# Attention block with a gated MLP on one core: VectorE's 32x32 turns for q's last 64 columns, and mean and scale of tiles 6 to 8 through DRAM

## The chip, the cores and the metric

The kernel runs on one core of one Trainium2 chip. A core has five engines that each work through a queue of their own in order: PE (TensorE, matrix products), DVE (VectorE), ACT (ScalarE), POOL (GpSimd) and SP (SyncE, which here issues nearly all DMAs). An instruction that waits for a semaphore holds up everything behind it on its engine. The metric is the time of one execution in microseconds (us); lower is better.

## The reference

The input x has 2048 rows of 576 numbers. Each row is normalized (mean and variance), then goes through two branches: a linear attention with 32 heads of 18 columns, and a gated MLP of width 4608. The output is x + s * silu(B).

```python
xn = (x - mean) / sqrt(var + 1e-5)
q, k, v = heads(xn @ wqkv)                        # 32 heads of 18
phi = lambda t: where(t > 0, t + 1, exp(t)) + 1e-6
kv  = einsum("hsd,hse->hde", phi(k), v);  z = sum over s of phi(k)
o   = (phi(q) @ kv) / (phi(q) . z + 1e-6)
s   = o @ wo
B   = (gelu(xn @ w_gate) * (xn @ w_up)) @ w_down
out = x + s * silu(B)
```

All of it is float32.

## The kernel before

The 2048 rows are cut into 16 tiles of 128 (n or t in the code) and into 4 blocks of 512 rows (tb, 4 tiles each, TT = 4). Matrix products of float32 are made as sums of products of two shorter words, "hi" (a rounded copy, made by ACT) and "lo" (the rest, made by DVE as source minus hi), so that each operand is cut once and PE runs 7 passes for one product.

The attention branch comes first and takes some 275 us; the MLP follows with a long run of matrix products. In the attention branch:

- `kv_tile(t)` makes tile t's 1152 columns of k and v (and, in the third of its three products, 64 columns of q) by three groups of 14 matmuls into banks `kv_0`, `kv_1`, `kv_2`. Between them it prepares tile t + 1: `turn` and `place`. Every second tile, `kv_pair` adds the last two tiles to the sum kv.
- For tiles 4 and up x is loaded already turned (columns on partitions). `spread` and `scales` work out mean and scale of a pair of tiles per row, with rows on partitions (tiles `bn`, `mv`, `st`). `normalize` (called by `place`) needs them with rows along the free dimension, the same on all partitions. Up to tile 8 `turn` gives this: two PE transposes of a broadcast column, into a bank `ms`. For tiles 9 and up `scales` writes four numbers per row to DRAM (`md`), a second DMA reads them back to all partitions (`mx`), and `sort_rows` has ACT copy them into order (`mr`).
- `normalize` is then a subtraction and two multiplications on DVE (tiles `x`, `xf_B`), two ACT copies (hi) and four DVE subtractions (lo) into `xo_B`, which the next tile's matmuls read.
- phi of q is needed with columns on partitions, in 5 groups of 128 rows (gi) for each block. Groups 0 to 3 come from 14 matmuls of 512 columns each (`q_mm`, bank `q_0` to `q_3`). Group 4 holds q's last 64 columns, which `v_post` has copied from `kv_2` into `qt`, twice side by side; four PE transposes turn them into bank `q_4`. Then `phi`: ACT makes relu(-q) (`e_q`), DVE makes max(q, 0) + eps (`ph`), ACT makes the exponential of `e_q`, POOL adds. In every `phi` DVE's step waits for ACT's first one, which reads the same bank.
- Blocks 0 and 1 store phi(q) to DRAM (`q_store`), blocks 2 and 3 keep it (`q_hold`). `den` sums the denominators of a block (PE), takes the reciprocal and spreads it into `aux` (DVE and ACT), and `scale` multiplies it in by a matmul (bank `b`).

What stands between the matmuls of q is set by the tables `behind` and `ahead`, keyed by (block, group): an entry runs after the matmuls and the phi of that group are issued. All compute instructions keep the order in which the code issues them; the pools hand out buffers in that order (`gl` has 6, `tmp` has 4, and `bank` has 6 PSUM banks).

Of the kernel before, what the change touches and what calls it, by code (L numbers as in the profile page):

```python
# [8 lines left out]
F32 = mybir.dt.float32  # L9
# [3 lines left out]
ALU = mybir.AluOpType  # L13
# [78 lines left out]
def block_kernel(ctx, tc, x, xe, xt, wq_d, wkv_d, wo, wgu_d, wd_d, out):  # L92
# [21 lines left out]
    def gl_tile(shape, name, dt=F32):  # L114
        return sb.tile(shape, dt, tag="gl", bufs=6, name=name)
# [6 lines left out]
    def act(*args, **kw):  # L122
        pin(nc.scalar.activation(*args, **kw))  # L123
# [61 lines left out]
    def scales(n0):  # L185

        n, mv, st = mom.pop(n0)
        v, r, c = (st[:, i, 0:n] for i in range(1, 4))
        if n == 1:
            vec("tensor_scalar", c, r, r, -0.5, op0=ALU.mult, op1=ALU.mult)  # L190
            vec("tensor_scalar", c, c, v, 1.5, op0=ALU.mult, op1=ALU.add)
            vec("tensor_scalar", c, c, r, None, op0=ALU.mult)
        else:
            vec("scalar_tensor_tensor", c, r, -0.5, r, op0=ALU.mult, op1=ALU.mult)
            vec("tensor_mul", c, c, v)
            vec("scalar_tensor_tensor", c, c, 1.5, r, op0=ALU.add, op1=ALU.mult)
        for t in range(n):
            scale_of[n0 + t] = mv[:, t, 0:1], c[:, t : t + 1]
        if n0 >= 2 * TT:
            vec("tensor_copy", st[:, 3, 2:4], mv[:, 0:2, 0])  # L200
            d = dr.tile([P, 4], F32, name=f"md_{n0}")
            mixed[n0] = g = gl_tile([P, P, 4], f"mx_{n0}")
            dma(out=d, in_=st[:, 3, :])
            dma(
                out=g.rearrange("p t c -> p (t c)"),
                in_=d.rearrange("t c -> (t c)")[None, :].to_broadcast([P, 4 * P]),
            )

    def sort_rows(n0):

        g = gl_tile([P, 4, P], f"mr_{n0}")
        act(g, mixed.pop(n0).rearrange("p t c -> p c t"), AF.Copy)
        for t in range(2):
            if n0 + t > 2 * TT:
                rows_of[n0 + t] = [g[:, None, i + t] for i in (2, 0)]

    def center(n):

# [267 lines left out]
    def v_post(t, c):  # L486

        if c == 1:
            vas[t] = slot([P, 2 * NHG, P // 2], F32, f"va_{t}")
            pool("memset", vas[t][:, :, 0:1], 1.0)  # L490
        va, src = vas[t], pkv[t, c]
        n = D - TW[0] if c == 1 else 0
        g = 4 * c - 4
        act(
            va[:, g : g + 4, 1 : GW // 2 + 1],
            src[:, n : n + 2 * GW].rearrange("p (g j) -> p g j", g=4), AF.Copy,
        )
        if c == 2:
            act(
                va[:, 8:10, 1 : W4 // 2 + 1],  # L500
                src[:, 2 * GW : 2 * GW + W4].rearrange("p (g j) -> p g j", g=2), AF.Copy,
            )
            tb, i = divmod(t, TT)
            if i == 0:
                qt[tb] = gl_tile([P, TT, 2, Q4], f"qt_{tb}")
            act(
                qt[tb][:, i], src[:, None, 2 * GW + W4 : TW[2]].to_broadcast([P, 2, Q4]), AF.Copy,
            )

    def run(todo, n=None):  # L510
        for _ in range(len(todo) if n is None else min(n, len(todo))):
# [36 lines left out]
    def q_mm(tb, gi, o):  # L548
        s, b = divmod(tb, 2)
        pq = bank(f"q_{tb}_{gi}")  # L550
        if gi == NHG - 1:
            t = qt.pop(tb)
            for i in range(TT):
                pin(nc.tensor.transpose(
                    pq[:, i * P : (i + 1) * P], t[:, i].rearrange("p r j -> p (r j)"), ident
                ))
        else:
            n = 0
            for j, nm in enumerate(BS[b]):
                for wi, xi, rows in PASSES:  # L560
                    mm(
                        pq, q_part(j, wi, slice(gi * P, (gi + 1) * P)), xo[s][nm][:, xi, :],
                        start=(n == 0), stop=(n == 2 * len(PASSES) - 1),
                    )
                    n += 1
        phi(o, pq, f"q{tb}_{gi}")

    def q_store(tb, gi):
        if tb not in ph_d:
# [908 lines left out]
    load_q(0)  # L1478
    for n in range(3, 2 * TT):
        ends = []  # L1480
        if n < 2 * TT - 2:
            ends.append(lambda n=n: x_next(n + 2))
        if n >= TT:
            j, c = divmod(n - TT, 2)
            prep_q(c, j)
# [8 lines left out]
            for nm in BS[0]:  # L1494
                keep(0, nm, xo[0][nm])
        if n == TT:
            q_store(0, 4)
        if n == TT + 3:
            keep(0, "B22", xo[0]["B22"])

# [19 lines left out]
    def form_apart(nm):  # L1520
# [12 lines left out]

    behind = {
        (0, 0): [
            lambda: kv_pair(N0), lambda: q_store(1, 4), lambda: spread(N0, 2),
            lambda: difference(0, 3),
        ],
        (0, 1): [lambda: scales(N0), lambda: form("T1")],
        (0, 2): [lambda: form_apart("T3")],  # L1540
        (0, 3): [lambda: turn(N0)],
        (1, 0): [lambda: place(N0)],
        (1, 1): [lambda: form("T2"), lambda: spread(N0 + 2, 2), lambda: scales(N0 + 2)],
    }
# [4 lines left out]
    for n in range(N0, 2 * N0):  # L1549
# [13 lines left out]
        if n == 2 * N0 - 1:  # L1563
# [128 lines left out]
```

## Time and profile before

| what | value |
|---|---|
| time, 3 runs | 1454.80, 1455.42 (median), 1455.93 us |
| profiled execution, its own time | 1454.71 us |
| its span in the profile | 1453.0 us |
| PE busy | 1446.4 us, 8272 matmuls |
| DVE, ACT, POOL busy | 1146.2, 565.5, 579.3 us |

The span is what the profile covers, from the first instruction to the last; the execution's time is 1.7 us more. In rows of the timeline the first number is the start in us, the second the length, then engine, line, operation, output <- inputs and shape; brackets at the end give the idle time before it and what ended it. The line numbers of most instructions are those of a helper (L129 matmul, L126 DVE, L123 ACT, L132 POOL, L135 DMA), so instructions are told apart by their tiles. The chain is the path that ended last, followed back from the end.

### The profile page before, as it was taken

Reading aid. Unit: us, or ns where it says so; the run is one execution under the profiler, and the core shown is the slowest. Engines: PE = TensorE matmul, PEld = TensorE weight load, DVE = VectorE, ACT = ScalarE, POOL = GpSimd, SP = SyncE. Lnnn points to the kernel's source line nnn. Section 1 sums busy time; section 2 is a strip of 40 time slices with the busy share of each in tenths; the row PEclk is TensorE's granted clock in tenths of the full one; section 3 lists DMA queues with packets and bytes.
Section 4 is the critical chain, followed back from the end, with each engine's and each line's share of the span. In section 5 each row is a group of like instructions: output and inputs, shape, how many; then the busy total and the mean of one; then the engine's idle time right before and its main releaser. Section 6 shows DMA issues by size and latency. Waiting matters only on the chain.

```text
span 1453.0 us, 22169 instructions
## 1 busy us (share of the span) xinstructions
PE 1446.4 (100%) x8272; PEld 1289.0 (89%) x8272; DVE 1146.2 (79%) x1609; ACT 565.5 (39%) x918; POOL 579.3 (40%) x520
## 2 busy tenths in 40 slices
PE   9999999999999999999999999999999999999998
PEld 8989989988888888888888888888889999999998
DVE  7688667376787887887777878777878978989898
ACT  6444365333232233322332232332236555545454
POOL 3342440225756567565575755667632000000000
PEclk9999999999999999999999999999999999999999
DMA  5554115621532315224242343324289887767886
GB/s 224 187 205 152 45 42 201 225 93 51 174 102 95 130 54 186 87 95 145 77 149 87 102 145 109 113 84 136 115 277 343 265 262 254 246 183 238 277 290 224
DMA packets 119237, 235.04 MB, mean 162 GB/s; under 512 B 11658, under 2 KB 45322, under 8 KB 117210
## 3 DMA queue, kind: packets, MB, share of 16 engines
q1 hardware_dynamic: 116330, 221.37, 45.2%
q0 software_dynamic: 2656, 12.06, 2.2%
q8 instruction: 65, 1.06, 0.3%
q14 instruction: 42, 0.34, 0.1%
q10 hardware_dynamic: 144, 0.20, 0.0%
HBM read 150.96 MB, written 82.58 MB: 161 GB/s over the span
## 4 chain that ended last, share of the span: by engine, by line
PE 97%; DVE 1%; ACT 1%; issue 0%; POOL 0%; DVEq 0%; ACTq 0%; POOLq 0%
PE bd L129 25%; PE al L887 16%; PE de L887 16%; PE ga L887 16%; PE kv L129 8%; PE be L887 8%; PE s L129 4%; PE q L129 3%; PE kv_a L129 1%; PE idle L129 0%; PE d L129 0%; PE kw L129 0%; PE b L129 0%; ACT e_q L123 0%; PE xt L241 0%
## 5 line engine op out<-in xcount | busy, mean ns | idle before, releaser
L132 POOL TENSOR_TENSOR sm<-raw 128x384 f32<-128x384 f32 x72 | 75.0, 1042 | 144.3 <-DMA raw<-in_wgu_dram 113.3
L129 PE MATMUL kv<-wkv,xo_B 128*128 128x412 f32 (+2 forms) x662 | 125.0, 347 | 0.3 <-ACT xo_B L123 0.3
L129 PEld LDWEIGHTS kv<-wkv,xo_B 128*128 128x128 f32 x662 | 120.3, 188 | 1.7 <-ACT xo_B L123 0.8
L126 DVE TENSOR_TENSOR wa<-sm,wa 128x768 fp32r<-128x768 f32 x72 | 92.2, 1281 | 36.1 <-ACT wa L123 35.2
L129 PE MATMUL bd<-w_head,hi 128*128 128x288 f32 x516 | 118.0, 294 | 0.0
L126 DVE TENSOR_TENSOR wb<-raw,wb 128x256 fp32r<-128x256 f32 (+1 forms) x108 | 101.2, 937 | 7.4 <-ACT wb L123 5.8
L126 DVE TENSOR_TENSOR wa<-raw,wa 128x256 fp32r<-128x256 f32 x72 | 65.6, 911 | 50.7 <-ACT wa L123 47.5
L123 ACT ACTIVATE hi<-raw_h 128x1024 fp32r<-128x1024 f32 x59 | 62.5, 1059 | 93.0 <-PE bd L129 56.5
L129 PE MATMUL bd<-w_end,hi 128*128 128x288 f32 x448 | 89.8, 294 | 0.0
L123 ACT ACTIVATE spot_h<-spot_h 128x512 f32<-128x512 f32 x49 | 30.8, 633 | 149.4 <-DVE spot_h L126 149.4
L129 PEld LDWEIGHTS bd<-w_head,hi 128*128 128x128 f32 x516 | 87.0, 188 | 0.1
L126 DVE TENSOR_TENSOR raw_h<-raw_h,hi 128x1024 fp32r<-128x1024 f32 x59 | 71.7, 1220 | 19.1 <-ACT hi L123 18.9
L129 PE MATMUL bd<-w_end,raw_h 128*128 128x288 f32 x264 | 77.9, 295 | 0.0
L123 ACT ACTIVATE wa<-sm 128x1152 fp32r<-128x1152 f32 x36 | 41.8, 1161 | 91.1 <-PE de L887 91.1
L123 ACT ACTIVATE u<-al 128x512 f32<-128x512 f32 x72 | 41.0, 592 | 89.9 <-PE al L887 68.1
L129 PEld LDWEIGHTS bd<-w_end,hi 128*128 128x128 f32 x448 | 71.8, 188 | 0.0
L129 PE MATMUL bd<-beside,raw_h 128*128 128x288 f32 x240 | 70.8, 295 | 0.0
L132 POOL TENSOR_TENSOR spot_h<-spot_h,spot_h 128x512 f32<-128x512 f32 x45 | 62.5, 1396 | 2.9 <-DVE spot_h L126 2.4
L887 PE MATMUL al<-xo_B,wa 128*128 128x512 f32 x252 | 63.0, 389 | 0.0
L887 PE MATMUL al<-xo_B,wb 128*128 128x512 f32 x252 | 63.0, 389 | 0.0
L887 PE MATMUL be<-xo_T,wa 128*128 128x512 f32 x252 | 63.0, 389 | 0.0
L887 PE MATMUL be<-xr_T,wa 128*128 128x512 f32 x252 | 63.0, 389 | 0.0
(278 smaller groups left out, 4036.0 us busy)
## 6 DMA issues: line engine op xcount, KB each, us to landing
raw_h<-hs SPq DMA_DIRECT2D x176, 256.0 KB
raw<-in_wgu_dram SPq DMA_DIRECT2D x36, 768.0 KB
hs<-spot_h SPq DMA_DIRECT2D x90, 256.0 KB
hs<-spot_g SPq DMA_DIRECT2D x80, 256.0 KB
b<-in_wd_dram SPq DMA_DIRECT2D x42, 432.0 KB
hs<-spot_m SPq DMA_DIRECT2D x38, 256.0 KB
raw_g<-hs SPq DMA_DIRECT2D x22, 256.0 KB
raw_a<-hs SPq DMA_DIRECT2D x20, 256.0 KB
```

What stands on the lines that cost most here:

```text
L123: pin(nc.scalar.activation(*args, **kw))
L126: pin(getattr(nc.vector, op)(*args, **kw))
L129: pin(nc.tensor.matmul(*args, **kw))
L132: pin(getattr(nc.gpsimd, op)(*args, **kw))
L887: nc.tensor.matmul(o, w[0:rows, wi, :], xop[0:rows, xi, :], start=(start and n == 0), stop=(n == len(PASSES) - 1), skip_group_check=True,)
```

## The change

The change has two parts.

First, q's last 64 columns are no longer turned on PE. `qt` keeps them once instead of twice. `last_phi` applies phi to a block's `qt` with rows on partitions (two DVE steps, one exponential on ACT, one addition on POOL, each on 256 columns). `last_turn` then turns them by 8 DVE transposes of 32 partitions and 4 x 32 columns, and has ACT copy the 64 resulting partitions to the other 64. `last_store` (blocks 0 and 1) and `last_hold` (blocks 2 and 3) call it, each some way behind `last_phi`.

Second, tiles 6, 7 and 8 get mean and scale through DRAM, as tiles 9 and up do already. For this `x_next(6)` runs at the end of tile 3 in place of tile 4, and `sort_rows(8)` stands behind group (0, 3) in place of `turn(8)`.

```diff
         for t in range(n):
             scale_of[n0 + t] = mv[:, t, 0:1], c[:, t : t + 1]
-        if n0 >= 2 * TT:
+        if n0 >= TT + 2:
             vec("tensor_copy", st[:, 3, 2:4], mv[:, 0:2, 0])
...
         for t in range(2):
-            if n0 + t > 2 * TT:
-                rows_of[n0 + t] = [g[:, None, i + t] for i in (2, 0)]
+            rows_of[n0 + t] = [g[:, None, i + t] for i in (2, 0)]
...
-                qt[tb] = gl_tile([P, TT, 2, Q4], f"qt_{tb}")
-            act(
-                qt[tb][:, i], src[:, None, 2 * GW + W4 : TW[2]].to_broadcast([P, 2, Q4]), AF.Copy,
-            )
+                qt[tb] = gl_tile([P, TT, Q4], f"qt_{tb}")
+            act(qt[tb][:, i], src[:, 2 * GW + W4 : TW[2]], AF.Copy)
...
     def q_mm(tb, gi, o):
...
-        if gi == NHG - 1:
-            t = qt.pop(tb)
-            for i in range(TT):
-                pin(nc.tensor.transpose(
-                    pq[:, i * P : (i + 1) * P], t[:, i].rearrange("p r j -> p (r j)"), ident
-                ))
...
+    def last_phi(tb):
+        t = qt[tb]
+        e = tmp([P, TT, Q4], f"e_q{tb}_l")
+        vec("tensor_scalar", e, t, 0.0, None, op0=ALU.min)
+        vec("tensor_scalar", t, t, 0.0, EPS, op0=ALU.max, op1=ALU.add)
+        act(e, e, AF.Exp)
+        pool("tensor_add", t, t, e)
+
+    def last_turn(tb, o):
+        t = qt.pop(tb)
+        cols = o.rearrange("p (i t) -> p i t", i=TT)
+        for c in range(0, Q4, 32):
+            for r in range(0, P, 32):
+                vec("transpose", cols[c : c + 32, :, r : r + 32], t[r : r + 32, :, c : c + 32])
+        act(o[Q4:P], o[0:Q4], AF.Copy)
+
+    def last_store(tb):
+        o = gl_tile([P, TBN], f"ph_{tb}_4")
+        last_turn(tb, o)
+        if tb not in ph_d:
+            ph_d[tb] = dr.tile([P, NHG, TBN], F32, name=f"phd_{tb}")
+        dma(out=ph_d[tb][:, NHG - 1, :], in_=o)
+
+    def last_hold(tb, i):
+        if tb not in ph:
+            ph[tb] = big(i, [P, NHG, TBN], F32, f"ph_{tb}")
+        last_turn(tb, ph[tb][:, NHG - 1, :])
...
     for n in range(3, 2 * TT):
         ends = []
-        if n < 2 * TT - 2:
-            ends.append(lambda n=n: x_next(n + 2))
+        if n == 3:
+            ends.append(lambda: x_next(6))
...
         if n == TT:
-            q_store(0, 4)
+            last_phi(0)
+        if n == TT + 1:
+            last_store(0)
...
     behind = {
         (0, 0): [
-            lambda: kv_pair(N0), lambda: q_store(1, 4), lambda: spread(N0, 2),
-            lambda: difference(0, 3),
+            lambda: kv_pair(N0), lambda: last_phi(1), lambda: spread(N0, 2),
+            lambda: difference(0, 3), lambda: last_store(1),
         ],
         (0, 1): [lambda: scales(N0), lambda: form("T1")],
         (0, 2): [lambda: form_apart("T3")],
-        (0, 3): [lambda: turn(N0)],
+        (0, 3): [lambda: sort_rows(N0)],
...
     ahead = {
         (2, 0): [
-            lambda: kv_pair(2 * N0), kv_done, lambda: q_hold(2, 7, 4), spread_sel,
-            lambda: difference(1, 3),
+            lambda: kv_pair(2 * N0), kv_done, lambda: last_phi(2), spread_sel,
+            lambda: difference(1, 3), lambda: last_phi(3),
         ],
         (2, 1): [lambda: kv_wo(4)],
-        (2, 2): [lambda: kv_wo(0), lambda: kv_wo(1), move_rows],
-        (2, 3): [lambda: kv_wo(2), lambda: kv_wo(3)],
-        (3, 0): [lambda: den(2), lambda: q_hold(3, 8, 4)],
+        (2, 2): [lambda: kv_wo(0), lambda: kv_wo(1), move_rows, lambda: last_hold(2, 7)],
+        (2, 3): [lambda: kv_wo(2), lambda: kv_wo(3), lambda: last_hold(3, 8)],
+        (3, 0): [lambda: den(2)],
```

How this stands in the engines' queues is shown at three places; in these rows the number at the end of a tile's name only tells one tile from another. The first is ACT's queue behind group 0 of block 0, before and then after (`e_q_0` is that group's, `e_q_1` the next one's, `st` belongs to `spread` of tiles 8 and 9, `xo_T` is the operand T1):

```order
L123 ACTIVATE e_q_0_958<-e_q_0_958 128x512
L123 ACTIVATE e_q_4_991<-q_4_986 128x512
L123 ACTIVATE e_q_4_991<-e_q_4_991 128x512
L123 ACTIVATE st_1005<-mv_998,eps_t 128x2
L123 ACTIVATE st_1005<-st_1005 128x2
L123 ACTIVATE e_q_1_1026<-q_1_1011 128x512
```

```order
L123 ACTIVATE e_q_0_963<-e_q_0_963 128x512
L123 ACTIVATE e_q_l<-e_q_l 128x256
L123 ACTIVATE st_1002<-mv_995,eps_t 128x2
L123 ACTIVATE st_1002<-st_1002 128x2
L123 ACTIVATE ph_4_1007<-ph_4_1007 64x512
L123 ACTIVATE e_q_1_1035<-q_1_1020 128x512
```

The copy of the turned columns (`ph_4`) now stands ahead of group 1's `e_q_1`, and the two steps on bank `q_4` are gone.

The second is ACT's queue around group 0 of block 1, before and after (`e_q_3` is the last group of block 0, `xo_B` belongs to tile 8):

```order
L123 ACTIVATE e_q_3_1095<-q_3_1080 128x512
L123 ACTIVATE e_q_3_1095<-e_q_3_1095 128x512
L123 ACTIVATE e_q_0_1120<-q_0_1105 128x512
L123 ACTIVATE e_q_0_1120<-e_q_0_1120 128x512
L123 ACTIVATE xo_B_1127<-xf_B_1128 128x3x128
```

```order
L123 ACTIVATE e_q_3_1104<-q_3_1089 128x512
L123 ACTIVATE e_q_3_1104<-e_q_3_1104 128x512
L123 ACTIVATE mr_1110<-mx_1046 128x512
L123 ACTIVATE e_q_0_1128<-q_0_1113 128x512
L123 ACTIVATE e_q_0_1128<-e_q_0_1128 128x512
L123 ACTIVATE xo_B_1135<-xf_B_1136 128x3x128
```

`mr`, which needs the second of the two DMAs, stood before in tile 8's `kv_tile`, thirteen instructions further on; now it stands ahead of block 1's first `e_q_0`.

The third is DVE's queue from `kv_wo(3)` to the reciprocal of `den(2)`, before and after (`kvl` belongs to `kv_wo`, `ph_2105` and `ph_2120` are phi(q) of block 3):

```order
L126 TENSOR_TENSOR kvl<-kw_0_2096,kvh 126x288
L126 TENSOR_TENSOR kvl<-kw_1_2098,kvh 126x288
L126 TENSOR_SCALAR ph_2105<-q_0_2106 128x512
L126 TENSOR_SCALAR r_2147<-d_2126 128x128
L126 RECIPROCAL r_2147<-r_2147 128x128
L126 TENSOR_TENSOR aux<-r_2147,aux 32x128 x4
L126 TENSOR_SCALAR ph_2105<-q_4_2158 128x512
```

```order
L126 TENSOR_TENSOR kvl<-kw_0_2111,kvh 126x288
L126 TENSOR_TENSOR kvl<-kw_1_2113,kvh 126x288
L126 STREAM_TRANSPOSE ph_2120<-qt_1679 32x4x32 x8
L126 TENSOR_SCALAR ph_2120<-q_0_2130 128x512
L126 TENSOR_SCALAR r_2171<-d_2150 128x128
L126 RECIPROCAL r_2171<-r_2171 128x128
L126 TENSOR_TENSOR aux<-r_2171,aux 32x128 x4
```

The last group's phi stood behind the reciprocal and `aux`; its 8 turns now stand ahead of them. The same 8 turns stand between `kv_wo(1)` and `ph` of group 3 in block 2, and in both places ACT's copy stands ahead of the next group's `e_q`. On PE the order of everything else is as it was: only the 16 transposes of `qt` and the 6 of tiles 6, 7 and 8 are gone.

More of the change, by code (lines that the diff above doesn't have):

```diff
@@ L550, in q_mm @@
         pq = bank(f"q_{tb}_{gi}")
-        if gi == NHG - 1:
-            t = qt.pop(tb)
-            for i in range(TT):
-                pin(nc.tensor.transpose(
-                    pq[:, i * P : (i + 1) * P], t[:, i].rearrange("p r j -> p (r j)"), ident
-                ))
[L557 to L565, printed above, removed]
-        phi(o, pq, f"q{tb}_{gi}")
+        n = 0
+        for j, nm in enumerate(BS[b]):
+            for wi, xi, rows in PASSES:
+                mm(
+                    pq, q_part(j, wi, slice(gi * P, (gi + 1) * P)), xo[s][nm][:, xi, :],
+                    start=(n == 0), stop=(n == 2 * len(PASSES) - 1),
+                )
+                n += 1
+        phi(o, pq, f"q{tb}_{gi}")
+    def last_phi(tb):
[22 more added lines that the diff above has]
+        last_turn(tb, ph[tb][:, NHG - 1, :])
     def q_store(tb, gi):
```

## The prediction

> **What bounds the kernel now.** I read the page's busy times and its chain first, then PE's timeline, then the timelines of DVE, ACT and SP wherever PE comes close to waiting. The first fence has the page's busy times, its chain by engine, one stretch of busy time (columns PE, PEld, DVE, ACT, POOL, then clock and DMA) and PE's only wait in the attention branch behind the start.
>
> ```profile
> PE 1446.4 (100%) x8272; PEld 1289.0 (89%) x8272; DVE 1146.2 (79%) x1609; ACT 565.5 (39%) x918; POOL 579.3 (40%) x520
> PE 97%; DVE 1%; ACT 1%; issue 0%; POOL 0%; DVEq 0%; ACTq 0%; POOLq 0%
> 77.00:98.00 21.00, 21.00 (x133) 17.68 (x132) 19.88 (x26) 11.81 (x22) 8.86 (x7) 1.00 0.20 72
> 114.61 10.64 PE L129 MATMUL kv<-wkv,xo_B 128*128 128x416 f32 x56 [0.30 <-ACT xo_B L123]
> ```
>
> PE is the bound, so a microsecond of matmuls saved is a microsecond of time, as long as nothing else comes later than PE does. There is one place where it already does: tile 9's matmuls wait 0.30 us for `xo_B`, and ahead of that DVE is busy 19.88 of 21 us. Around 110 us DVE and PE are tied, and PE's savings up to there are worth nothing unless DVE gets faster too.
>
> **What is removed.** The chain gives the transposes' steps on PE's path: four groups on `qt` (q) and, of the five on mean and scale (ms), the three of tiles 6, 7 and 8.
>
> ```profile
> 53.52 0.44 PE q L554 x4
> 56.59 0.22 PE ms L233 x2
> 65.90 0.36 PE ms L233 x2
> 83.52 0.59 PE q L554 x4
> 93.64 0.22 PE ms L233 x2
> 178.35 0.59 PE q L554 x4
> 197.88 0.58 PE q L554 x4
> ```
>
> They come to 2.20 + 0.80 = 3.00 us, 0.21% of the time: 1.83 us ahead of tile 9 (of it 1.02 before 80 us), 1.17 behind it. That is all the change can win on PE, and a change of 0.2% (2.9 us) is about what a measurement of this kernel can tell from none.
>
> **What a block of 8 turns costs (T).** No row shows a DVE transpose. Nearest are rows of few columns: two independent steps of 160 columns in sequence, one of 416, and groups (count, busy us, mean ns) of 32 partitions by 128 columns, one undisturbed and one that shares its time with POOL's additions.
>
> ```profile
> 43.49 0.32 DVE L126 TENSOR_SCALAR e_k<-kv 128x160 f32<-128x160 f32 x1
> 43.73 0.32 DVE L126 TENSOR_SCALAR pk<-kv 128x160 f32<-128x160 f32 x1
> 46.79 0.59 DVE L126 TENSOR_SCALAR e_k<-kv 128x416 f32<-128x416 f32 x1 [2.74 <-PE kv L129]
> L126 DVE TENSOR_TENSOR aux<-r,aux 32x128 fp32r<-32x128 f32 x16 | 4.5, 283 | 2.3 <-ACT aux L123 1.7
> L126 DVE TENSOR_TENSOR wa<-raw,wa 32x128 fp32r<-32x128 f32 x36 | 36.7, 1018 | 1.1
> ```
>
> From below: (0.59 - 0.32) / 256 = 1.05 ns a column with no fixed part, 8 x 128 columns, 1.1 us. From above: 8 x 0.283 = 2.3, and 0.7 more for one turn that meets POOL (1018 against 283 ns), 3.0 us. I take the distance of the two 160-column steps, 0.24, as nearest for independent steps: T = 8 x 0.24 = 1.9 us.
>
> [...]
>
> **Place A: block 1's turns, and mean and scale of tile 8.** Rows of DVE, then ACT, then SP (DMA issues), and the DMA traffic in GB/s from 142 to 152 us in quarters of a microsecond.
>
> ```profile
> 84.78 0.69 DVE L126 TENSOR_SCALAR ph<-q 128x512 f32<-128x512 f32 x1 [0.51 <-ACT e_q L123]
> ...
> 87.48 1.75 DVE L126 TENSOR_TENSOR xf_B<-xf_B,xf_B 128x1536 f32<-128x1536 f32 x1
> 89.14 0.68 DVE L126 TENSOR_SCALAR ph<-q 128x512 f32<-128x512 f32 x1
> ...
> 91.20 0.16 DVE L126 COPY st<-mv 128x2 f32<-128x2 f32 x1
> ...
> 97.78 0.69 DVE L126 TENSOR_SCALAR ph<-q 128x512 f32<-128x512 f32 x1 [0.20 <-ACT e_q L123]
> ```
>
> ```profile
> L123 ACT ACTIVATE e_q<-e_q 128x512 f32<-128x512 f32 x20 | 12.7, 633 | 0.6
> ...
> 97.15 0.60 ACT L123 ACTIVATE e_q<-q 128x512 f32<-128x512 f32 x1 [2.14 <-PE q L129]
> ...
> 110.86 1.13 ACT L123 ACTIVATE mr<-mx 128x512 f32<-128x512 f32 x1
> ```
>
> ```profile
> 91.70 0.38 SPq L135 DMA_DIRECT2D md<-st  x1
> 94.91 0.32 SPq L135 DMA_DIRECT2D mx<-md  x1
> ...
> 109.34 0.32 SPq L135 DMA_DIRECT2D md<-st  x1
> 110.82 0.32 SPq L135 DMA_DIRECT2D mx<-md  x1
> ...
> 145.98 0.34 SPq L135 DMA_DIRECT2D mx<-md  x1
> ...
> GB/s 0 0 0 0 0 0 0 0 0 0 8 0 0 0 0 0 0 0 0 25 147 188 188 148 164 139 49 66 0 0 0 0 0 0 0 0 0 0 0 0
> ```
>
> DVE reaches the turns, where it starts `ph` of group 1 at 89.14 now, at 87.6: 1.02 sooner with PE's lead, and 0.5 because `ph` of group 4 with its wait (0.51 + 0.61 to the next step) gives way to two 256-column steps of about 0.3. The turns end at 87.6 + T. Then comes the costly step: ACT's copy of 64x512 (0.63, like the other 512-column copies) stands ahead of `e_q` of group 1 (0.60), and DVE's `ph` waits for that. `ph` starts at 88.9 + T with 0.07 of gaps, with DVE idle for 1.3. From `ph`'s start to the end of `scales` takes 91.36 - 89.14 = 2.2: 91.1 + T. SP issues `md` 0.34 later, `mx` 1.48 to 3.21 later (the two pairs above), the read lasts about 3.0 (issue at 145.98, traffic until 149.0), and `mr` takes 1.13. Behind it, `e_q` of block 1's first group starts at 97.1 to 98.8 + T, against 97.15 now. So A = T + 0.8 = 2.7, between T - 0.2 (DVE's own queue, which then decides) and T + 1.7. From 97.15 on to tile 9's `xo_B` the chain runs through ACT and DVE alone, so 114.61 moves by A. PE arrives at 114.31 - 1.83 = 112.5 and waits some 4.8 us, and its 1.83 are lost.
>
> The early part I cost at nothing. `spread` and `scales` of tiles 6 and 7, some 3 us of DVE, move from the end of tile 4 to the end of tile 3, where DVE idles 2.74 (row at 46.79); their two ACT steps then stand ahead of tile 3's last copies of v, which `kv_pair` needs at about 47.0, a tie worth 0.3 at most. `md` and `mx` go through SP ahead of the load of tiles 8 and 9, which is held back in any case:
>
> ```profile
> 50.75 0.37 SPq L135 DMA_DIRECT2D x<-in_x_dram  x1
> ```
>
> so `mx` has from about 47.5 until tile 5's `kv_tile`, some 8 us, to land, and block 0's store, now a tile later, holds up nothing that is needed before the MLP. Block 0's turns fall between tiles 5 and 6, where DVE has the same idle time (now free of `spread`). POOL gets four additions of 256 columns for four of 512.
>
> **Place B: blocks 2 and 3.** Rows of DVE, and the chain's row of the first `scale` of block 2 (b).
>
> ```profile
> 189.23 1.02 DVE L126 TENSOR_TENSOR kvl<-kw,kvh 126x288 fp32r<-126x288 f32 x2
> 192.21 0.69 DVE L126 TENSOR_SCALAR ph<-q 128x512 f32<-128x512 f32 x1 [1.97 <-ACT e_q L123]
> ...
> 194.30 1.02 DVE L126 TENSOR_TENSOR kvl<-kw,kvh 126x288 fp32r<-126x288 f32 x2
> 197.38 0.69 DVE L126 TENSOR_SCALAR ph<-q 128x512 f32<-128x512 f32 x1 [2.06 <-ACT e_q L123]
> ...
> 199.69 1.28 DVE L126 TENSOR_TENSOR aux<-r,aux 32x128 fp32r<-32x128 f32 x4 [0.44 <-ACT aux L123]
> ...
> 201.66 0.45 PE b L129 x2
> ```
>
> DVE's idle 1.97 and 2.06 could hold a block of turns each, were it not for ACT's copy and `e_q` behind each (1.3 with gaps). `kvl` ends at 190.25 now, and some 0.8 later after: `last_phi(3)` puts two DVE steps and an exponential ahead of group 1's `e_q` (0 to 1.2). Then `ph` of group 3 starts at 191.05 + T + 1.3; from `ph` to the end of the next `kvl` takes 195.32 - 192.21 = 3.1, the second turns and copy T + 1.3, from `ph` of block 3's first group to the end of `aux` 200.97 - 197.38 = 3.6. So `aux` is ready at 200.4 + 2T = 204.2, where PE now starts `scale` at 201.66 and would come 1.17 sooner. B = 2T - 1.25 = 2.55, between 0.95 and 4.75; PE's 1.17 are lost here too. Behind that PE leads again, so nothing is won back.
>
> **The sum.** Places A and B come to 3T - 0.45 = 5.25 us slower; with both ends of T and of the DMAs 1.85 to 9.45. The profiled execution took 1454.71 (span 1453.0 and 1.7 around it), 0.7 below the median of the runs, 1455.42. So 1460.0 beside the profiled one, 1460.7 beside the median.
>
> **Rivals.**
> - *All hidden, faster.* PE stays the bound throughout because ACT and DVE have slack that the named releasers hide: 1455.4 - 3.0 = 1452.4. For it speaks that ACT is busy only 39%. Against it: it needs 4.5 us of slack between 97.15 and 114.61, where the row at 114.61 shows PE already late by 0.30. It decides at tile 9's `xo_B`: if that is there by 112.5, this holds.
> - *Only A costs.* B's two blocks fit into the idle 1.97 and 2.06, if T is near 1.1 and the 0.8 is not there (2T - 2.05 = 0.15, about the measurement of nothing): A at 1.1 + 0.8 less up to 1.17 gives +0.7 to +2.1, some 1456.8, within 0.2%.
> - *PE's clock drops in the waits.* The first rows of PE's timeline show that after idleness PE starts slow: 18 matmuls of a transpose's size took 4.21 us (0.23 each), later 6 took 0.85 (0.14 with the pipeline's end).
>
> ```profile
> 1.59 4.21 PE L129 MATMUL idle<-ident 128*128 128x128 f32 x18 [1.59 <-POOL ident masks.py:199]
> ...
> 6.94 0.85 PE L241 MATMUL xt<-ident,x 128*128 128x128 f32 x6 [0.28 <-PE idle L129]
> ```
>
> If a wait of 4.8 us brings that back, half speed over 4.2 us costs 2.1: 1462.8. Against it: the longest wait behind the start is 0.30, so no row shows such a wait and what follows. [...]
>
> **How the numbers follow.** Forecast (both places cost) 0.58; clock drop 0.10; only A 0.20; all hidden 0.12. The time is that of the forecast, 1460.7. The range reaches up to the sum's upper bound, 1455.4 + 9.45 = 1464.9, and down to 1454.0, which takes in the third case and leaves out the faster one; the forecast's own range is 1457.3 to 1464.9. Slower by over 0.2% means above 1458.3: forecast and clock drop, less 0.03 for a small T, 0.65. Faster by over 0.2% is the all-hidden case, 0.12, and 0.23 are left.
>
> **What would show it.** In the profile after: PE waits for `xo_B` at tile 9 for about 4.8 us and for `aux` at b of block 2 for about 3.7; 8 transposes take about 1.9 us; ACT's `ph` copy ends just ahead of `e_q`; `mr` waits for the DMA. If `xo_B` is in time at tile 9, or a turn takes under 0.1 us, or ACT's copy is done before PE's group is, the forecast is wrong.

## The result, and the profile after

The changed kernel takes 1468.39 us (median of 4 runs, 1467.88 to 1469.09) against 1455.51 for the kernel before on the same chip: 1.0088 times as long, 95% interval 1.0076 to 1.0100. That is slower, as forecast, but by 12.9 us instead of 5.25; it lies 3.5 us above the top of the range (1464.9). The profiled execution has a span of 1466.2 us, 13.2 more than before. A second set of runs gave 1467.97 and the ratio 1.0086 (1.0071 to 1.0102).

The page after has PE still busy nearly all the time, but the chain is no longer PE's alone: DVE now has 4% of it instead of 1%, and DMA 1%.

```profile
PE 1448.4 (99%) x8250; PEld 1289.0 (88%) x8250; DVE 1169.1 (80%) x1646; ACT 565.3 (39%) x919; POOL 578.8 (39%) x520
...
PE 93%; DVE 4%; ACT 1%; issue 1%; DMA 1%; SPq 0%; ACTq 0%; DVEq 0%
```

PE's waits in the attention branch (what waited, for what, us in total, times, longest), then the rows of PE's timeline at the places of the waits:

```profile
PE kv L129 <- ACT xo_B L123: 7.1, 2, 5.9
PE b L129 <- DVE aux L126: 4.0, 1, 4.0
PE kw L129 <- DVE kv L126: 0.4, 1, 0.4
```

```profile
106.30 7.98 PE L129 MATMUL kv<-wkv,xo_B 128*128 128x416 f32 x42 [1.14 <-ACT xo_B L123]
120.21 12.76 PE L129 MATMUL kv<-wkv,xo_B 128*128 128x416 f32 x56 [5.92 <-ACT xo_B L123]
...
212.96 0.70 PE L129 MATMUL b<-aux 128*128 128x512 f32 x2 [4.00 <-DVE aux L126]
```

The waits are where places A and B were put: for `xo_B` at tile 9 (forecast 4.8, measured 5.92, and 1.14 more at tile 8 ahead of it) and for `aux` at block 2's first `scale` (forecast 3.7, measured 4.00). What was not forecast is the length of the row at 120.21: the same 56 matmuls took 10.64 before and 12.76 now. In half microseconds (columns: window, its length, PE busy, granted clock, DMA share, GB/s) the clock stands at half speed for a while around each wait:

```profile
117.50:118.00 0.50, 0.00 (x0) 1.00 0.00 0
118.00:118.50 0.50, 0.00 (x0) 0.50 0.41 29
...
124.50:125.00 0.50, 0.50 (x3) 0.68 1.09 436
125.00:125.50 0.50, 0.50 (x5) 1.00 0.60 240
...
213.00:213.50 0.50, 0.50 (x3) 1.00 0.00 0
213.50:214.00 0.50, 0.50 (x3) 0.57 0.00 0
...
216.50:217.00 0.50, 0.50 (x3) 0.52 0.00 0
217.00:217.50 0.50, 0.50 (x4) 1.00 0.00 0
```

Where the time comes from follows from four starts on PE, before and after:

| start on PE | before | after | later by | gained since the row above |
|---|---|---|---|---|
| tile 9 | 114.61 | 120.21 | 5.6 | 5.6: place A |
| block 2's first q | 173.7 | 181.0 | 7.3 | 1.7: half clock behind tile 9 |
| block 2's first `scale` (b) | 201.66 | 212.96 | 11.3 | 4.0: place B |
| first matmul of the MLP (al) | 276.6 | 289.8 | 13.2 | 1.9: mostly half clock behind `scale` |

Of the last 1.9 us, 1.6 are the 14 matmuls of q behind that `scale` (4.80 us instead of 3.17 in the chain). The MLP itself is as long as before. Place A in the rows of DVE, then POOL, then ACT, then the chain's steps of the two DMAs:

```profile
83.72 1.35 DVE L126 TENSOR_SCALAR qt<-qt 128x256 f32<-128x256 f32 x1
...
88.75 2.50 DVE L126 STREAM_TRANSPOSE ph<-qt 32x128 f32<-32x128 f32 x8
92.57 0.69 DVE L126 TENSOR_SCALAR ph<-q 128x512 f32<-128x512 f32 x1 [1.32 <-ACT e_q L123]
...
104.17 2.00 DVE L126 TENSOR_TENSOR xf_B<-x,mr 128x384 f32<-128x384 f32 x2
```

```profile
103.28 2.00 POOL L132 TENSOR_TENSOR ph<-ph,e_q 128x512 f32<-128x512 f32 x1 [0.54 <-DVE ph L126]
```

```profile
91.28 0.63 ACT L123 ACTIVATE ph<-ph 64x512 f32<-64x512 f32 x1 [3.74 <-DVE ph L126]
91.94 0.60 ACT L123 ACTIVATE e_q<-q 128x512 f32<-128x512 f32 x1
...
100.82 1.12 ACT L123 ACTIVATE mr<-mx 128x512 f32<-128x512 f32 x1 [2.47 <-DMA mx<-md]
101.85 0.57 ACT L123 ACTIVATE e_q<-q 128x512 f32<-128x512 f32 x1
```

```profile
95.14 2.10 DMA md<-st
97.25 3.48 DMA mx<-md
```

The steps stand as forecast: 8 turns, ACT's copy, `e_q`, DVE idle for 1.32; the two DMAs; `mr` waiting for them, and `e_q` of block 1 behind it at 101.85 instead of 97.15. A block of 8 turns takes 2.50 us, not 1.9. Place B in DVE's rows has the same pattern twice:

```profile
198.64 2.49 DVE L126 STREAM_TRANSPOSE ph<-qt 32x128 f32<-32x128 f32 x8
202.46 0.69 DVE L126 TENSOR_SCALAR ph<-q 128x512 f32<-128x512 f32 x1 [1.32 <-ACT e_q L123]
...
205.47 2.49 DVE L126 STREAM_TRANSPOSE ph<-qt 32x128 f32<-32x128 f32 x8
209.28 0.69 DVE L126 TENSOR_SCALAR ph<-q 128x512 f32<-128x512 f32 x1 [1.32 <-ACT e_q L123]
...
211.53 1.28 DVE L126 TENSOR_TENSOR aux<-r,aux 32x128 fp32r<-32x128 f32 x4 [0.37 <-ACT aux L123]
```

### The profile page after: what moved, and what is told of

Same layout as the page of the kernel before. It is cut to its first block, busy times and chain, and to the rows that moved or that the text cites. A ratio compares the mean times of both kernels' runs of the same rounds, so it can differ in the third digit from the quotient of the medians.

```text
span 1466.2 us, 22167 instructions
## 1 busy us (share of the span) xinstructions
PE 1448.4 (99%) x8250; PEld 1289.0 (88%) x8250; DVE 1169.1 (80%) x1646; ACT 565.3 (39%) x919; POOL 578.8 (39%) x520
## 4 chain that ended last, share of the span: by engine, by line
PE 93%; DVE 4%; ACT 1%; issue 1%; DMA 1%; SPq 0%; ACTq 0%; DVEq 0%
PE bd L129 25%; PE ga L905 16%; PE al L905 16%; PE de L905 16%; PE kv L129 8%; PE be L905 8%; PE s L129 4%; DVE ph L126 1%; PE q L129 1%; DVE xf_B L126 1%; ACT e_q L123 1%; PE kv_a L129 1%; PE b L129 0%; DVE bn L126 0%; PE d L129 0%
## 5 line engine op out<-in xcount | busy, mean ns | idle before, releaser
L126 DVE TENSOR_TENSOR wb<-raw,wb 128x256 fp32r<-128x256 f32 (+1 forms) x108 | 106.0, 981 | 7.2 <-ACT wb L123 5.6
L126 DVE TENSOR_TENSOR wa<-raw,wa 128x256 fp32r<-128x256 f32 x72 | 69.1, 959 | 50.7 <-ACT wa L123 49.6
L905 PE MATMUL ga<-xo_B,wb 128*128 128x512 f32 x252 | 63.1, 390 | 0.0
L905 PE MATMUL ga<-xr_B,wb 128*128 128x512 f32 x252 | 63.0, 389 | 0.0
L905 PE MATMUL al<-xr_B,wa 128*128 128x512 f32 x252 | 63.0, 389 | 0.0
```

The source lines that it names most:

```text
L126: pin(getattr(nc.vector, op)(*args, **kw))
L905: nc.tensor.matmul(o, w[0:rows, wi, :], xop[0:rows, xi, :], start=(start and n == 0), stop=(n == len(PASSES) - 1), skip_group_check=True,)
```

## The experiments

The kernel before took 1456.13, 1455.66, 1455.45 and 1455.69 us beside the four groups of runs; each run below is given by its ratio to those that ran with it, with the 95% interval.

**One part alone: the turns.** Tiles 6 to 8 get mean and scale as in the kernel before.

```diff
-        if n0 >= TT + 2:
+        if n0 >= 2 * TT:
...
-        (0, 3): [lambda: sort_rows(N0)],
+        (0, 3): [lambda: turn(N0)],
```

> Only the turns of q's last 64 columns go to VectorE; mean and scale of tiles 6 to 8 stay on PE. In the changed kernel DVE's 512-column step of block 0's group 1 came at 92.57 against 89.14 before, 3.43 later, and the DMAs and `mr` then held block 1's first such step from about 101.2, where DVE's own queue would have let it start, to 102.45. Theory (the turns and the copy carry place A, the DMAs add the rest): tile 9 starts 5.60 - 1.25 = 4.35 us later than before; the wait again halves PE's clock (1.85); place B and its clock drop are as in the changed kernel (4.0 + 1.8): +12.0, some 1467.5. Rival (the wait for `mr` carries place A, the turns alone fit in): tile 9 starts less than 2 us later, with no clock drop there, some 1461 to 1463.

Measured: 1464.92 us, ratio 1.0062 (1.0045 to 1.0079). Tile 9 starts at 118.70, 4.1 later than before (4.35 expected), and place B is as in the changed kernel. The span is 3.4 us below that kernel's, more than the 1.25 of the DMAs: tile 9 starts 1.5 sooner than there, and in this profile the clock did not drop at tile 9. PE's waiting there is split in two.

```profile
PE ms L233 <- DVE st L126: 2.4, 1, 2.4
PE kv L129 <- ACT xo_B L123: 2.2, 1, 2.2
```

```profile
116.00:118.00 2.00, 0.54 (x4) 1.00 0.40 82
118.00:120.00 2.00, 1.30 (x7) 1.00 1.03 330
```

So the turns carry most of place A's wait, and the theory holds but for the clock: waits of 2.4 us (until 95.73) and 2.2 us (until 118.70), with over 20 us of matmuls between them, leave it alone here.

**One part alone: mean and scale through DRAM.** q's last columns stay on PE.

```diff
-        if n0 >= 2 * TT:
+        if n0 >= TT + 2:
...
-        (0, 3): [lambda: turn(N0)],
+        (0, 3): [lambda: sort_rows(N0)],
```

> Only mean and scale of tiles 6 to 8 go through DRAM; q's last columns are turned on PE as before. From the end of `scales` to the end of `mr` the changed kernel took 101.94 - 94.99 = 6.95; counted from 91.36 before this ends at 98.3, where block 1's first `e_q` had started at 97.15. Theory: tile 9 starts 1.15 later, PE's 0.44 of tiles 6 and 7 are lost in the wait (some 1.9 in all), place B is as before, and the clock stays at 1.00 because the wait is short: some 1456.6. Rival (the DMAs are the main cost): tile 9 starts 3 or more later and the clock drops: 1460 or more. Rival (hidden): 1455.4 or below.

Measured: 1459.34 us, ratio 1.0018 (1.0009 to 1.0028), between the theory and its first rival. Tile 9 starts 2.5 later, not 1.15, and the clock drops after a wait of 3.1. PE, then ACT, then DVE, then two of the half microseconds:

```profile
117.14 13.31 PE L129 MATMUL kv<-wkv,xo_B 128*128 128x416 f32 x56 [3.10 <-ACT xo_B L123]
```

```profile
97.72 1.11 ACT L123 ACTIVATE mr<-mx 128x512 f32<-128x512 f32 x1 [2.76 <-DMA mx<-md]
98.74 0.59 ACT L123 ACTIVATE e_q<-q 128x512 f32<-128x512 f32 x1
```

```profile
101.07 2.00 DVE L126 TENSOR_TENSOR xf_B<-x,mr 128x384 f32<-128x384 f32 x2
```

```profile
116.00:116.50 0.50, 0.00 (x0) 0.65 0.98 188
...
122.50:123.00 0.50, 0.50 (x3) 0.52 0.18 49
```

`e_q` is late by 98.74 - 97.15 = 1.6, and the multiplications into `xf_B` took 2.00 where they had taken 1.02: together 2.6, the delay of tile 9. The 13.31 against 10.64 are the clock, at 0.50 until 123.0. That drop does not come every time: of the ten executions two took 1457.27 us, 2.1 below the median and 0.7 from the theory's time. One of these has a mean granted clock of 1.000, so no such drop; the profiled one, with 6.8 us at half speed, has 0.998. The parts alone cost 9.8 and 4.8 us of span, both in one kernel 13.2: they share the wait at tile 9.

**Why `xf_B` doubled.** In the kernel before the factor lay in PSUM (`ms`), now it lies in SBUF (`mr`), and POOL's addition of a phi runs at that time in both. The run above, without that one addition:

```diff
-        pool("tensor_add", o, o, e)
+        if name != "q1_0":
+            pool("tensor_add", o, o, e)
```

> The kernel with only mean and scale through DRAM, and without POOL's addition in the phi of block 1's group 0 (so phi of 128 of q's columns lacks the exponential's part). In that kernel's trace the two multiplications into `xf_B` of tile 8, which read `mr` in SBUF, took 2.00 us beside that addition (itself 2.00); where they read `ms` in PSUM, in the kernel before and with the turns alone, they took 1.02 beside the same addition (itself 1.27). Theory (two operands in SBUF and POOL's addition hinder each other, and that is part of the price of sending mean and scale through DRAM): `xf_B` 1.02, tile 9 0.98 earlier, its wait 2.1 instead of 3.1 and so too short to halve PE's clock: about 0.98 + 2.3 less, 1456.0. Rival (reading `mr` itself is slow, or the first use of it): `xf_B` stays at 2.00, time within 1 us of 1459.3.

Measured: 1456.47 us, ratio 1.0007 (0.9997 to 1.0016): 0.8 us above the kernel before beside it, where the run above was 3.2 above its own.

```profile
101.57 1.03 DVE L126 TENSOR_TENSOR xf_B<-x,mr 128x384 f32<-128x384 f32 x2
```

```profile
116.68 10.65 PE L129 MATMUL kv<-wkv,xo_B 128*128 128x416 f32 x56 [2.19 <-ACT xo_B L123]
```

Both halves of the theory came out: 1.03 for `xf_B`, a wait of 2.19, and the 56 matmuls back at 10.65. So the two multiplications took 2.00 only with `mr` in SBUF and the addition beside them: 1.02 with `ms` in PSUM and the addition, 1.03 with `mr` and without it. By what the two hinder each other was not shown.

**PE kept busy in the waits.** Matmuls of the identity that feed nothing stand ahead of tile 9 and ahead of block 2's first `scale`, first 40 and 26 of them:

```diff
+    spare = own_bank("spare")
+
+    def keep_busy(n):
+        for _ in range(n):
+            mm(spare[:, 0:P], ident, ident, start=True, stop=True)
...
+        if n == N0 + 1:
+            keep_busy(40)
...
-        (3, 1): [lambda: scale(2, 0, 1), lambda: halve(2, 0, 1)],
+        (3, 1): [lambda: keep_busy(26), lambda: scale(2, 0, 1), lambda: halve(2, 0, 1)],
```

> The changed kernel with 40 matmuls of the identity put into PE's wait ahead of tile 9 and 26 into that ahead of block 2's first `scale`; they feed nothing and by 0.117 us each (half of the 0.23 at the slow start) fill 4.7 of 5.9 and 3.0 of 4.0 us. Theory (idleness halves PE's clock, and it costs some 3.7 us behind the two waits): clock 1.00 throughout, the two waits end where they did, about 3.7 faster than the changed kernel: 1464.7. Rival (the slow stretch is not from idleness, or half of PE's work is enough to be hidden): 1468.4 as the changed kernel, with PE's clock at 0.50 in the same places or the waits ending later.

Measured: 1470.32 us, ratio 1.0098 (1.0083 to 1.0113). The clock stayed at 1.00 in both places, but the time did not fall: each of these is two of the profile's matmuls, and the 80 outlasted the wait by some 3 us.

```profile
114.54 9.09 PE L129 MATMUL spare<-ident 128*128 128x128 f32 x80
123.39 6.91 PE L129 MATMUL kv<-wkv,xo_B 128*128 128x416 f32 x36
```

With 22 and 14:

> As the run with PE kept busy, but with 22 and 14 matmuls of the identity instead of 40 and 26: there each was two of the profile's matmuls, 80 of them took 9.09 us where the wait was 5.92, so PE came out later than the wait would have ended. 44 by 0.111 us are now 4.9 of the 5.9 us ahead of tile 9, and 28 are 3.1 of the 4.0 ahead of block 2's first `scale`. Theory (idleness halves the clock): clock 1.00 throughout, the waits end where they did, 1.9 and 1.8 us faster behind them: 3.7 below the changed kernel, 1464.7. Rival (the last microsecond of the wait is enough, or DVE and ACT are late behind the waits anyway): within 1 us of the changed kernel, 1468.

Measured: 1466.32 us, ratio 1.0074 (1.0060 to 1.0087), less gain than the 3.7 expected.

```profile
114.69 5.07 PE L129 MATMUL spare<-ident 128*128 128x128 f32 x44
120.77 10.63 PE L129 MATMUL kv<-wkv,xo_B 128*128 128x416 f32 x56 [1.01 <-ACT xo_B L123]
```

The waits end where they did (120.77, against 120.60 in the changed kernel's next trace), the 56 matmuls take 10.63, the clock is 1.00 in the attention branch, and the MLP's first matmul comes at 286.9 against 289.9. So in these two waits the clock halved with PE idle and not with PE busy for 5.07 of 6.1 us and 3.29 of 4.2, and the two drops cost 3.0 us up to the MLP's start. Of these the span kept 2.2 (1463.8 against 1466.0); the stretch behind is 0.8 longer, which no run explains, and the medians differ by 1.7, with intervals of about 2 us to either side.

**The changed kernel once more.**

> The changed kernel once more, beside these runs on the same chip. All theories: 1468.4 within 1 us, the waits 5.9 and 4.0 us and the halved clock behind each as in its first profile; if the early part (tiles 4 to 7) moves by half a microsecond from one execution to the next, tile 8's wait for `xo_B` shows it.

Measured: 1467.97 us, ratio 1.0086 (1.0071 to 1.0102); waits 5.89 and 4.00, the clock at half speed behind both. Tile 8's wait was 1.47 against 1.14 and tile 9 started 0.4 later: differences of half a microsecond between starts of two kernels say nothing.

**`mr` behind `e_q`.**

```diff
-        (0, 3): [lambda: sort_rows(N0)],
-        (1, 0): [lambda: place(N0)],
+        (1, 0): [lambda: sort_rows(N0), lambda: place(N0)],
```

> The changed kernel with ACT's copy of mean and scale of tile 8 (`mr`) moved behind block 1's first phi, so that only `normalize` of tile 8 waits for it. Theory (what stands behind the waiting instruction on ACT is part of the price): DVE's step of block 1's group 0 no longer waits and runs at about 101.2; `x` of tile 8 starts at about 101.95 against 103.17: 1.2 faster, 1467.2, the wait at tile 9 4.7. Rival (the DMAs' landing alone sets it, or POOL's addition then falls on DVE's long steps): 1468.4, no change.

Measured: 1468.89 us, ratio 1.0088 (1.0073 to 1.0103): the rival. DVE's step of group 0 no longer waited (1.23 in the changed kernel), but `mr` still had to wait for the DMA (until 101.70, 100.82 in the changed kernel, whose early part ran 0.6 sooner), and POOL's additions lay on `x` as well (1.26 against 0.96). Tile 9 started at 120.19 against 120.21. The four executions fall into two pairs, 1467.7 and 1467.8 (mean clock 0.996 and 0.997) and twice 1470.0 (0.995): in the profiled one, of the slower pair, half speed behind `scale` lasted 6.8 us (211.6 to 218.5) instead of the changed kernel's 3.4. No gain is to be measured from freeing what stands behind the waiting `mr` on ACT; the DMAs' landing sets the place.

**ACT's copy behind the next `e_q`.** `last_copy` holds the copy of the turned 64 partitions (for block 1 with its store) and runs after the next group's phi is issued.

```diff
-        (0, 1): [lambda: scales(N0), lambda: form("T1")],
+        (0, 1): [lambda: last_copy(1), lambda: scales(N0), lambda: form("T1")],
...
-        (2, 3): [lambda: kv_wo(2), lambda: kv_wo(3), lambda: last_hold(3, 8)],
-        (3, 0): [lambda: den(2)],
+        (2, 3): [
+            lambda: last_copy(2), lambda: kv_wo(2), lambda: kv_wo(3), lambda: last_hold(3, 8),
+        ],
+        (3, 0): [lambda: last_copy(3), lambda: den(2)],
```

> The changed kernel with ACT's copy of the turned 64 partitions put behind the next group's two steps on ACT, for blocks 1, 2 and 3 (block 1's store to DRAM goes with it). Theory (a third of the price is the coupling: copy 0.63 and `e_q` 0.60 between the turns and DVE's next step, which idled 1.32 each time): DVE's step starts 1.32 earlier at each of the three places: tile 9 1.3 earlier (wait 4.6, clock still halved), `aux` 2.6 earlier, the wait for it 4.0 - 2.6 = 1.4, too short to halve the clock (two waits of 2.2 and 2.4 did not, one of 3.1 did), another 1.7: 1468.4 - 1.3 - 2.6 - 1.7 = 1462.8. Rival (DVE's queue is long anyway, and what is won is lost to POOL's additions or to the DMAs behind `scales`): within 1.5 us of the changed kernel, 1467 or more.

Measured: 1464.95 us, ratio 1.0063 (1.0049 to 1.0076). Place B did what the theory says: the wait for `aux` fell from 4.0 to 1.4 and the clock stayed at 1.00 there. Place A gained nothing (tile 9 at 120.19). DVE's `ph` came 1.28 sooner (91.29), but `mx` could not be issued sooner than before, at 97.25. SP's rows, which hold the issues:

```profile
94.33 0.40 SPq L135 DMA_DIRECT2D md<-st  x1
97.25 0.32 SPq L135 DMA_DIRECT2D mx<-md  x1
```

`md` took 2.9 us instead of 2.1. Its 2 KB now stand behind two stores of 256 KB, since block 1's turned group is stored later: the traffic from 94.0 to 96.0 is 172, 406, 410 and 82 GB/s in half microseconds, some 535 KB, where the changed kernel has 352 and 193 from 95.5 to 96.5, one store. That the stores held `md` up fits this, but was not tested by itself.

**Turns alone, copies behind.** The edits of the first run and of the last one together, which takes the DMAs out of place A.

> Turns alone (mean and scale of tiles 6 to 8 on PE) and ACT's copies behind the next group's steps. With the DMAs gone from place A, the 1.32 us of the copy and `e_q` should come through there, as they did at place B. Theory: tile 9 starts 4.09 - 1.3 = 2.8 later than before, no wait long enough to halve the clock, `scale` of block 2 another 1.5 later as in the run with the copies behind: 1455.6 + 4.3 = 1459.9. Rival (place A is not shortened by the copy, since something else ends last there): tile 9 3.5 or more later, 1461 or more.

Measured: 1459.85 us, ratio 1.0031 (1.0018 to 1.0043), in accord with the theory. Tile 9 starts 2.7 late, and in the profiled execution (1459.03 us) PE's waits are 1.1, 2.2 and 1.4 and the mean clock is 1.000. With the DMAs gone the 1.3 of copy and `e_q` do come through at place A. That the median lies within 0.1 us of the forecast is partly luck: the median execution and the slowest, 1461.94, have a mean clock of 0.998, so the clock dropped somewhere in them, and two executions without a drop took 1459.0.

**The turns where DVE idles.** Tile 8 on PE again, tiles 6 and 7 through DRAM; block 2's phi and turns in tile 12, block 1's in tile 13, block 3's phi behind `move_rows` and its copy behind the next `e_q`. An extract of the edit, without the room for the moved tiles:

```diff
-            lambda: kv_pair(N0), lambda: last_phi(1), lambda: spread(N0, 2),
-            lambda: difference(0, 3), lambda: last_store(1),
+            lambda: kv_pair(N0), lambda: spread(N0, 2), lambda: difference(0, 3),
...
+        if n == 2 * N0 - 4:
+            late_ = [lambda: last_phi(2)]
+            ends += [lambda: last_turn(2, gl_tile([P, TBN], "ph_2_4")), lambda: last_copy(2)]
+        if n == 2 * N0 - 3:
+            late_ = [lambda: last_phi(1)]
+            ends += [lambda: last_store(1), lambda: last_copy(1)]
```

> Turns stay on VectorE, but where DVE idles: block 0's as in the changed kernel, block 1's and 2's phi and turns in tiles 12 and 13 (block 1's `qt` and block 2's turned rows have room of their own), block 3's phi behind `move_rows`, its turns where they are, with ACT's copy behind the next `e_q`. Tile 8 gets mean and scale by PE's transposes again; tiles 6 and 7 through DRAM. Theory (the price is where the turns and the DMA wait stand, not the turns): ahead of tile 9 DVE's queue loses group 4's step (0.69 and its wait of 0.51), tile 9 comes up to 1.2 earlier than before; `aux` is 0.4 late, less than PE's gain of 0.6 ahead of it: 1454.0 (1453.3 to 1455.5), no wait of PE over 2 us and clock 1.00. Rival (20 us of DVE transposes and their POOL neighbours cost wherever they stand): 1458 or more.

Measured: 1462.51 us, ratio 1.0048 (1.0036 to 1.0061): the rival's time, but not for its reason. Places A and B went as expected (tile 9 1.07 sooner than before, `aux` just in time). The loss is new, at the start of tile 14, where PE waits for what tiles 12 and 13 should have made (1.7 for `xo_B`, then the two waits below). DVE, ACT and PE:

```profile
162.28 2.50 DVE L126 STREAM_TRANSPOSE ph<-small 32x128 f32<-32x128 f32 x8 [2.12 <-POOL small L132]
```

```profile
164.81 0.63 ACT L123 ACTIVATE ph<-ph 64x512 f32<-64x512 f32 x1 [4.25 <-DVE ph L126]
165.46 0.50 ACT L123 ACTIVATE va<-kv 128x252 f32<-128x252 f32 x2
```

```profile
161.63 0.47 PE L129 MATMUL kv_a<-pk,va 128*64 128x72 f32 x8 [0.64 <-POOL va L132]
165.90 0.99 PE L129 MATMUL kv_a<-pk,va 128*64 128x72 f32 x16 [3.80 <-ACT va L123]
```

The turns follow too closely on their own phi: DVE stood 2.12 for POOL's addition, ACT 4.25 in its copy for the turns, and `va`, which PE needs, behind that copy. In the 3.80 the clock halved again (0.50 from 163.5 to 170.3).

**And one DVE step less ahead of tile 9.** The same, with the subtraction for operand T4 moved from block 0's group 0 to tile 9, its cut into words to tile 10 (extract).

```diff
-            lambda: kv_pair(N0), lambda: spread(N0, 2), lambda: difference(0, 3),
+            lambda: kv_pair(N0), lambda: spread(N0, 2),
...
+        if n == N0 + 1:
+            ends.append(lambda: difference(0, 3))
```

> As the run with the turns apart, and DVE's subtraction for the operand T4 (1.75 us) moved from block 0's group 0 to the end of tile 9, its cut into words to tile 10. Theory (ahead of tile 9 DVE is the bound, and PE's 1.8 us of savings there are worth something only if DVE gets lighter): tile 9 another 0.6 to 1.7 earlier: 1453.0 (1452.0 to 1454.5). Rival (what leaves that stretch delays tiles 10 and 11, where DVE is busy 7.5 and 8.0 of 9 us): no gain over the run with the turns apart.

Measured: 1465.43 us, ratio 1.0066 (1.0053 to 1.0080): the rival, and worse. Tile 9 came no sooner (113.67 against 113.54), since DVE now idled for 1.22 where the 1.75 us had stood:

```profile
87.03 0.69 DVE L126 TENSOR_SCALAR ph<-q 128x512 f32<-128x512 f32 x1 [1.22 <-ACT e_q L123]
```

and tile 12 got a wait of 0.98 for `xo_B` that was not there.

**Phi, turns and copy a tile or more apart.** As the run with the turns where DVE idles, but block 1's phi in tile 10, its turns in tile 12, its copy ahead of tile 13; block 2's in 13, 14 and ahead of 15 (extract).

```diff
+        if n == 2 * N0 - 6:
+            late_ = [lambda: last_phi(1)]
+        if n == 2 * N0 - 4:
+            late_ = [lambda: last_turn(1, big(12, [P, TBN], F32, "ph_1_4"))]
+        if n == 2 * N0 - 3:
+            last_copy(1)
+            late_ = [lambda: last_phi(2)]
+        if n == 2 * N0 - 2:
+            late_ = [lambda: last_turn(2, at["t4"])]
+        if n == 2 * N0 - 1:
+            last_copy(2)
```

> As the run with the turns apart, but phi, turns and ACT's copy each a tile or more from the next, so that no step waits for the one before it: block 1's phi in tile 10, its turns in tile 12, its copy ahead of tile 13; block 2's in tiles 13, 14 and ahead of 15 (its turned rows and block 1's lie in room that is free then). In that run tile 9 came 1.07 earlier than before and `scale` of block 2 followed block 2's first q 0.6 sooner, but DVE idled 2.1 for POOL's addition ahead of the turns in tiles 12 and 13, ACT's copy stood ahead of `mr` and `va`, and PE waited 1.7, 0.6 and 3.8 us with its clock halved behind. Theory (the price is the order in the queues, not the turns): these waits go, the gains stay: 1455.5 - 1.07 - 0.6 = 1453.8 (1453.2 to 1455.5), clock 1.00, no wait of PE over 0.5 us. Rival (turns of 2.5 us do not fit into a tile's idle time of DVE): PE still waits at tile 13 or 14, 1457 or more.

Measured: 1454.45 us, ratio 0.9992 (0.9984 to 1.0001), 13.5 us below the changed kernel beside it. All its waits on PE in the attention branch:

```profile
PE kv L129 <- ACT xo_B L123: 0.3, 1, 0.3
PE kv_a L129 <- ACT va L123: 0.2, 1, 0.2
PE b L129 <- DVE aux L126: 0.2, 1, 0.2
```

The mean clock of the profiled execution is 1.000 and the 32 turns take 2.5 us a block as ever. Against the kernel before the gain of 1.0 us is at the edge of what can be measured; tile 9 (114.04 against 114.61) and the MLP's start (275.9 against 276.6) are 0.6 and 0.7 earlier, though 2.8 us of PE's transposes are gone here too (all but tile 8's 0.22): the rest goes at the ties with `xo_B` and `aux`, where PE still waits. So the turns need not cost anything. With the first run the price can be parted: tile 8 has its mean and scale from PE in both, and there the turns in their old order cost 9.8 us of span, here none. That much is the order in the queues; the other 3.4 of the 13.2 came with the way of mean and scale through DRAM, about half of it as the clock behind tile 9's wait.

## Why the prediction was right or wrong

The direction and both places were right: tile 9's `xo_B` through the turns, the copy ahead of `e_q` and `mr` behind two DMAs; `aux` through two more blocks of turns with their copies. That the early part costs nothing was right as well: the first wait behind the start is tile 8's, at 106.30, inside place A. And PE's 3.00 us were lost, as said. What failed is the size, and most of it by three terms: the clock, which the sum left out (3.0 to 3.6 us), POOL at place A, put at nothing (about 2), and T (1.8). By steps:

- **T, the duration of a block of turns.** Forecast 1.9, "nearest for independent steps"; measured 2.50. The distance of two independent 160-column steps is the wrong neighbour: the turns run at 0.30 us each with no overlap, like the upper bound's row (0.283), and start every 0.31. In the sum 3T this is 1.8 us.
- **Place A, "T + 0.8".** Measured 5.6, above the bound T + 1.7. With T at 2.50 the formula gives 3.3. Of the other 2.3, POOL has about 2: `qt`'s second step took 1.35 (83.72 to 85.07) where 0.3 was forecast (POOL's addition of a phi runs beside it, from 83.63 to 84.92; in blocks 0 and 2 the step took 0.29 to 0.30; this was not tested by itself), and `xf_B` 2.00 instead of 1.02, which the run without the addition shows. The prediction followed where mean and scale come from and when, not that DVE's operand thereby moves from PSUM into SBUF. The DMAs took what was forecast: from the end of `scales` to `mr` 5.8 us, within the 4.8 to 6.6 of its terms.
- **The rival "PE's clock drops in the waits", chance 0.10.** It came true, at both waits. It was priced at 2.1 for one wait, an estimate from the slow start's 4.21 us; the matmuls behind tile 9 took 12.76 - 10.64 = 2.1 longer. That the two agree is luck: half speed lasted 6.8 us there, not 4.2, and part of it passed while PE still stood. By the table the two drops make 3.6 us of the 13.2, and the run with PE kept busy took 3.0 of them away. The evidence against it ("the longest wait behind the start is 0.30") was no evidence: a kernel that never waits cannot show what a wait does. The forecast itself named waits of 4.8 and 3.7, and on those the slow start was the only row that bore. Even that row tells of half speed by its length alone: 18 matmuls in 4.21 us, where 44 of that shape took 5.07 in the run with 22 and 14, while the profile's clock column has 1.00 there (2 to 6 us). What sets the moment of the drop and the length of half speed was not shown: it lasted 6.8 us at tile 9 (118.0 to 124.8), from 3.7 us into the wait, and 3.4 us at `scale` (213.6 to 217.0), from 0.6 us after the wait had ended (212.96); with mean and scale alone through DRAM the drop came 2.1 us into a wait of 3.1.
- **Place B, "2T - 1.25".** With T at 2.50 this gives 3.75; measured 4.0. The step was right, its size was T's. That PE would come 1.17 sooner was not: it reached the first `scale` 27.96 us after block 2's first q, as before (27.97). What the transposes saved went at `kw` (0.9), whose 8 matmuls of groups 0 and 1 took 2.62 to the next q instead of 1.73 (0.45 of it a wait for DVE; that DVE is late there by block 3's early phi is read from its queue and was not tested).

Together: 5.25, and 1.8 for T, about 2 for POOL, 3.6 for the clock, make 12.7 of 13.2. The remaining 0.5 is not traced. The range's upper end took in T and the DMAs at their worst, but no clock drop; the rival with the drop stood on the middle of the sum (1460.7 + 2.1) and had it once. A longer T and longer waits were never put together with a drop at each.

## What to carry to other kernels

What work costs on an engine that is off the critical path depends on its place in the queue: the same 32 turns on DVE, busy for 80% of the span, cost 9.8 us of span ahead of steps that PE needs with a copy chained behind them, 13.2 with the two DMAs as well, and nothing where each step stands a tile away from the one that it waits for. Whoever forecasts a wait of PE of 3 us or more in a kernel like this one should price the clock behind it as part of that wait: in the profiled executions those of 3.1 to 5.9 us halved it, and tile 9's matmuls took 1.9 to 2.8 us longer. And where a change moves an operand of DVE from PSUM to SBUF, POOL's work at that time belongs in the sum (here 1.02 us became 2.00).

## What the runs showed of the hardware

- PE's clock: in the profiled executions waits of 1.1 to 2.4 us left it at 1.00, and waits of 3.1, 3.8, 4.0 and 5.9 us halved it to 0.50 each time. Other executions of the same kernels suggest that this is no sharp limit, though their waits are not on record: one of the kernel whose profile has the wait of 3.1 has a mean clock of 1.000, and two of the kernel with the turns alone and the copies behind, whose profile has no wait over 2.2, have 0.998. The drop came 1.4 to 5.2 us after PE went idle (at 163.5 with a wait from 162.10, close behind one of 0.64, in the run with the turns where DVE idles; at 116.15 with one from 114.04, at 119.5 with one from 114.30), and half speed then lasted 3.4 or 6.8 us. Tile 9's matmuls took 1.9 to 2.8 us longer, not in proportion to the wait: 2.7 behind one of 3.1, 2.1 behind one of 5.9.
- A DVE transpose of 32 partitions by 4 x 32 columns took 0.289 to 0.305 us in fp32, one after the other without overlap (8 in 2.50).
- Two multiplications with both operands in SBUF took 2.00 us beside POOL's addition, which itself took 2.00; 1.03 without it; and 1.02 with one operand in PSUM and the addition beside them.
